# One run of k^T v instead of two, the output weights loaded behind it, and the weight product spread over three q units

## The chip, the cores and the metric

The kernel runs on one core of one Trainium2 chip. The metric is the device time of one execution in microseconds (us), on the slowest core (here the only one). Whole runs of one and the same kernel scatter by about 1 us of 1,624 us.

Some words used throughout: PE is the tensor engine (matmul), PEld its weight loads, DVE the vector engine, ACT the scalar engine, SP the engine that issues all data transfers (DMA) here. PSUM is the memory that matmuls write.

## The reference, cut to what matters

```python
def A(x, wqkv, wo):                      # linear attention, S = 2048, D = 1024, 32 heads of 32
    q, k, v = split(x @ wqkv)
    phi = lambda t: where(t > 0, t + 1, exp(t)) + 1e-6
    kv  = einsum("bhsd,bhse->bhde", phi(k), v)          # one 32 x 32 matrix per head
    den = einsum("bhqd,bhd->bhq", phi(q), phi(k).sum(s)) + 1e-6
    o   = einsum("bhqd,bhde->bhqe", phi(q), kv) / den
    return merge_heads(o) @ wo
def B(x, w_gate, w_up, w_down):          # bilinear block, F = 3584
    return ((x @ w_gate) * (x @ w_up)) @ w_down
# x = x + A(layernorm(x)); x = x + B(layernorm(x)); and both once more (the same weights)
```

## The kernel before: the parts that matter

An attention layer is reordered. v is never computed. Instead G = x^T phi(k) is formed in eight chunks m of 128 rows ("g units", 32 full-size matmuls each), and k^T v is `wv^T G`, done per pair of heads with small matmuls on 64-column tiles of the array ("kv units"). Then M = kv * wo is formed for all heads with 32x32 tiles, in four "quarters" ("weight product"), and the output is q M / den ("out units", 16 full-size matmuls each). A "q unit" is 16 full-size matmuls for one tile of 128 tokens; `div_unit` divides q by den on DVE and turns it with a transposing DMA.

```python
Gs = [GL[:, 2 * D:3 * D], GL[:, 3 * D:4 * D], G3[:], W3[:, 3 * D:4 * D]]
Gs += Gs[0:3] + [pq[7]]                       # eight chunks of G share five places
# ... cut ...
def kv_unit(i):                               # i = 0: chunks 0-3, inside g unit 4; i = 1: chunks 4-7, later
    for m in range(4 * i, 4 * i + 4):
        for c in range(KD):
            for p in (0, 64):
                nc.tensor.matmul(out=acc[0][p:p + 64, c, :], lhsT=wkv[:, m, a:a + 64], rhs=Gs[m][:, a:a + 64], ...)
# ... cut ...  the weight product, in the middle of q units 14 and 15
steps(0, 0, 2);  quarter(0, 0)                # 4 full-size matmuls, then 16 small ones
steps(0, 2, 5);  quarter(0, 1)                # 6, then 16
steps(0, 5, 8);  steps(1, 0, 1);  quarter(1, 0)
phi(q unit 14);  steps(1, 1, 5);  quarter(1, 1)
steps(1, 5, 8);  phi(q unit 15)
# ... cut ...  the order around it (d = division of a tile, g and q = g and q units)
do([g[4]] + d(5, 6) + [q[1], g[5]] + d(7))
load_o(0, 4)                                  # output weights, lower half, 1 MB
load_o(4, 7)                                  # upper half but its last slice
do(d(8) + [q[2], g[6]] + d(9, 10) + [q[3]] + d(11) + [q[4]] + d(12) + [g[7], q[5], kv_unit(1)])
load_o(7, 8)                                  # last slice, 256 KB: its place held chunk 7 of G
last_q_with_m(later)
```

Of the kernel before, what the change touches and what calls it, by code (L numbers as in the profile page):

```python
# [12 lines left out]
F32 = mybir.dt.float32  # L13
# [13 lines left out]
def kernel(  # L27
# [11 lines left out]
    nc = tc.nc  # L39
# [46 lines left out]
    zacc = GL[:, 0:2 * D].bitcast(F32)  # L86
    G3 = const.tile([P, D], BF16, tag="G3", name="G3")

    Gs = [GL[:, 2 * D:3 * D], GL[:, 3 * D:4 * D], G3[:], W3[:, 3 * D:4 * D]]
    Gs += Gs[0:3] + [pq[7]]  # L90
    ring = [rows(R2[:, i * KD * NB:(i + 1) * KD * NB], NB) for i in range(4)]
    ring += [rows(W1[:, i * KD * NB:(i + 1) * KD * NB], NB) for i in range(2)]
    dn = [rows(PQ[0][:], D), rows(PQ[1][:], D), rows(W2[:, 0:4 * D], D), rows(W2[:, 4 * D:8 * D], D),
# [31 lines left out]
    def load_o(a, b):  # L125
        load(rows((W3 if a < 4 else PQ[1])[:], D)[:, a % 4:a % 4 + b - a, :], wo_v[:, a:b, :])
# [30 lines left out]
    def mm_tile():  # L157
        return psum.tile([P, 2, NB], F32, tag="mm", bufs=3, name="ps")
# [15 lines left out]
    def ln_stats(t):  # L174
        st = small.tile([P, 2, 6], F32, tag="st", name="st")
        for c in range(2):
            nc.vector.bn_stats(out=st[:, c, :], in_=X[:, t, c * NB:(c + 1) * NB])  # L177
        mv = small.tile([P, 2], F32, tag="mv", bufs=NT, name="mv")
        nc.vector.bn_aggr(out=mv[:], in_=st[:])  # L179
        ve = small.tile([P, 1], F32, tag="ve", name="ve")  # L180
        nc.gpsimd.tensor_scalar(out=ve[:], in0=mv[:, 1:2], scalar1=1e-5, scalar2=None, op0=ALU.add)  # L181
        rstd = small.tile([P, 1], F32, tag="rstd", bufs=NT, name="rstd")
        nc.gpsimd.tensor_tensor(out=rstd[:], in0=ve[:], in1=mhalf[:], op=ALU.pow)  # L183
        stat[t] = (mv, rstd)
# [11 lines left out]
    def both(ps, lhsT, rhs, start, stop):  # L196
        for n in range(2):
            nc.tensor.matmul(out=ps[:, n, :], lhsT=lhsT, rhs=rhs[:, n * NB:(n + 1) * NB], start=start, stop=stop)  # L198

    def phi(ps, dst, scale, later=None):  # L200
        e = small.tile([P, D], BF16, tag="eb", bufs=3, name="e")
        sc = {} if scale is None else {"scale": scale}
        nc.scalar.activation(out=e[:], in_=flat(ps), func=ACT.Exp, **sc)  # L203
        nc.scalar.activation(out=dst, in_=flat(ps), func=ACT.Relu, **sc)

        def sum_up():
            nc.vector.tensor_scalar(out=e[:], in0=e[:], scalar1=1.0, scalar2=EPS, op0=ALU.min, op1=ALU.add)  # L207
            nc.vector.tensor_tensor(out=dst, in0=dst, in1=e[:], op=ALU.add)

        if later is None:  # L210
            sum_up()
        else:
            later.append(sum_up)

    def layer_A(li):
# [3 lines left out]
        def scale_of(t):  # L219
            return stat[t][1][:] if first and t < TPG else None  # L220
# [14 lines left out]
            return lambda: k_part(t, 0, KD)  # L235

        def q_slot(t):
            return pq[t if t < 8 else t % 4]

        def q_unit(t, later=None):  # L240
            def run():
                ps = mm_tile()
                tl = t % TPG
                for k in range(KD):
                    both(ps, xT[t // TPG][:, k, tl * P:(tl + 1) * P], wq[:, k, :], k == 0, k == KD - 1)
                phi(ps, q_slot(t), scale_of(t), later)
            return run
# [43 lines left out]
        def g_unit(m):  # L291
            def run():
                ps = mm_tile()
                for t in range(NT):
                    both(ps, XN[:, t, m * P:(m + 1) * P], PK[:, t, :], t == 0, t == NT - 1)
                if m == 4:
                    kv_unit(0)()
                nc.scalar.copy(out=Gs[m], in_=flat(ps))
            return run

        acc = []

        def kv_unit(i):

            def run():
                if i == 0:
                    acc[:] = [psum.tile([P, KD, 64], F32, tag="kv0", bufs=1, name="kv")]
                for m in range(4 * i, 4 * i + 4):
                    for c in range(KD):
                        for p in (0, 64):  # L310
                            a = c * P + p
                            nc.tensor.matmul(out=acc[0][p:p + 64, c, :], lhsT=wkv[:, m, a:a + 64],  # L312
                                             rhs=Gs[m][:, a:a + 64], start=(m == 0 and c == 0),
                                             stop=(m == KD - 1), tile_position=(0, p), skip_group_check=True)
                if i == 1:
                    nc.vector.tensor_copy(out=KVb[:], in_=acc[0][:])
            return run

        def last_q_with_m(later):


            qs = [mm_tile(), mm_tile()]
            wide = mm_tile()
            bank = [psum.tile([P, NB], F32, tag=f"kv{i}", bufs=1, name="pm") for i in range(2)]

            def steps(i, a, b):
                t = 14 + i
                tl = t % TPG
                for c in range(a, b):
                    both(qs[i], xT[t // TPG][:, c, tl * P:(tl + 1) * P], wq[:, c, :], c == 0, c == KD - 1)  # L330

            def quarter(h, n, two):
                for i in range(4):
                    for j in range(4):
                        o = bank[j][DH * i:DH * i + DH, :] if j < 2 else two[DH * i:DH * i + DH, j - 2, :]
                        e = DH * (j % 2)
                        nc.tensor.matmul(out=o, lhsT=KVb[DH * j:DH * j + DH, 4 * h + i, e:e + DH],  # L337
                                         rhs=wo[4 * h + i][DH * j:DH * j + DH, n * NB:(n + 1) * NB],
                                         start=True, stop=True, tile_position=(DH * j, DH * i))

                def take(copy, r):
                    cols = slice(n * NB, (n + 1) * NB)
                    if r < 2:
                        copy(out=M[:, 4 * h + r, cols], in_=bank[r][:])
                    else:
                        copy(out=M[:, 4 * h + 2:4 * h + 4, cols], in_=two[:])
                return take

            dve, act = nc.vector.tensor_copy, nc.scalar.copy
            steps(0, 0, 2)  # L350
            take = quarter(0, 0, qs[1])
            take(dve, 0)
            take(dve, 1)
            take(act, 2)
            steps(0, 2, 5)
            take = quarter(0, 1, wide)
            take(dve, 0)
            take(dve, 1)
            take(act, 2)
            steps(0, 5, 8)  # L360
            steps(1, 0, 1)
            take = quarter(1, 0, wide)
            take(act, 0)
            take(act, 1)
            take(dve, 2)
            phi(qs[0], q_slot(14), scale_of(14), later)
            steps(1, 1, 5)
            take = quarter(1, 1, wide)
            take(dve, 0)
            take(dve, 1)  # L370
            take(dve, 2)
            do(later)
            steps(1, 5, 8)
            phi(qs[1], q_slot(15), scale_of(15))

        def out_unit(t):
            def run():
                ps = mm_tile()
                tl = t % TPG
                for c in range(KD):  # L380
                    both(ps, xT[t // TPG][:, c, tl * P:(tl + 1) * P], M[:, c, :], c == 0, c == KD - 1)
                nc.vector.tensor_tensor(out=X[:, t, :], in0=X[:, t, :], in1=flat(ps), op=ALU.add)  # L382
            return run

# [11 lines left out]
        if first:  # L396
# [16 lines left out]
            def take(copy, t, h, a, b):  # L413
                copy(out=xT[0][:, a:b, t * P:(t + 1) * P], in_=pts[t, h][:, a:b, :])  # L414
# [70 lines left out]
        def d(*ts):  # L485
            return [div_unit(t) for t in ts]

        g, q = ([f(i) for i in range(KD)] for f in (g_unit, lambda i: q_unit(8 + i)))
        later = []
        q[5] = q_unit(13, later)  # L490
        do([g[0], g[1]] + d(0) + [g[2]] + d(1, 2) + [g[3]] + d(3) + [q[0]] + d(4))
        do([g[4]] + d(5, 6) + [q[1], g[5]] + d(7))
        load_o(0, 4)
        load_o(4, 7)
        do(d(8) + [q[2], g[6]] + d(9, 10) + [q[3]] + d(11) + [q[4]] + d(12) + [g[7], q[5], kv_unit(1)])
        load_o(7, 8)
        last_q_with_m(later)
        load_gu(0)
        load_gu(1)
        load_gu(2)  # L500
        for j in DN_ORDER[:2]:
            load_dn(j)
        do([out_unit(0)] + d(13) + [out_unit(1), out_unit(2)] + d(14) + [out_unit(3), out_unit(4)] + d(15))
        for j in DN_ORDER[2:6]:
            load_dn(j)
        fill = [lambda t=t: ln_stats(t) for t in range(4)] + [b_norm(t) for t in range(4)]
        do(weave([out_unit(t) for t in range(5, NT)], fill))
        load_dn(DN_ORDER[6])


# [50 lines left out]
    def do(units):  # L561
        for u in units:
            u()
# [80 lines left out]
```

## Time and profile before

| | |
|---|---|
| median of the runs before the prediction | 1623.66 us (1623.50 to 1624.11, 3 runs) |
| span of the profiled run | 1622.4 us |
| PE busy | 99% |
| full-size (128x512) matmuls | 7,424 (28 of them, of the last tile, are cut in two), one start per 0.216 us: an estimated 1,603 us |

From the page of the kernel before: the span, the busy time by engine, and the chain of work that ended last.

```profile
span 1622.4 us, 18054 instructions
PE 1609.2 (99%) x7718; PEld 735.2 (45%) x7869; DVE 615.5 (38%) x941; ACT 283.8 (17%) x383; POOL 54.5 (3%) x135
PE 99%; issue 1%; DMA 0%; DVE 0%; ACT 0%; SPq 0%
```

PE is busy nearly always and the chain never leaves it. What remains to be won is the time in which PE is busy but off its pace of 0.216 us per full-size matmul. The timeline of PE shows it at the first kv unit (columns: start, duration, engine, line, operation, tiles, shapes, count):

```profile
129.14 0.69 PE L312 MATMUL kv<-GL,W 128*64 128x64 bf16 x32
129.67 0.42 PE L312 MATMUL kv<-G,W 128*64 128x64 bf16 x16
129.93 0.42 PE L312 MATMUL kv<-W,W 128*64 128x64 bf16 x16
130.28 3.63 PE L198 MATMUL ps<-W,xT 128*128 128x512 bf16 x15
```

The same kernel's second half of k^T v, from the timeline, starts at 168.37:

```profile
168.37 0.69 PE L312 MATMUL kv<-GL,W 128*64 128x64 bf16 x32
```

Records of the trace carry nanoseconds, and starts are worth more than durations (ends of matmuls are modelled). From them: the last full-size matmul before a kv unit starts 0.309 us ahead of the first small one, 0.093 more than the pace; two small ones take 0.0317 us, the first two 0.053 (0.049 is the step from the second start to the third); from the last small one to the first full-size one it is 0.128 us, and the step after that is 0.226. A half of k^T v (32 pairs) so costs 1.24 us, of which about 0.22 us is for going in and out.

The second quarter of the weight product starts with a wait; the timeline before, PE:

```profile
172.24 0.47 PE L337 MATMUL pm<-W,KVb 32*32 32x512 bf16 x2
172.34 0.39 PE L337 MATMUL ps<-W,KVb 32*32 32x512 bf16 x2
```

The first group lasts 0.47 us instead of 0.39: its second matmul starts 0.097 us after the first instead of 0.003. In the timeline of DVE the copies of the first quarter's two banks run from 170.99 to 172.28 us: the second matmul waits for DVE to empty its bank.

**The measure used from here on.** Whole runs scatter more than the change is worth, so I measure a stretch in each attention layer: from the start of the first matmul of the first g unit to the start of the first matmul of the first out unit. It holds everything that the change reorders ahead of the output stage. In the kernel before, these are the four starts, from the timeline of PE (first layer, then second):

```profile
91.06 1.24 PE L198 MATMUL ps<-R,R 128*128 128x512 bf16 x5
178.40 0.81 PE L198 MATMUL ps<-R,xT 128*128 128x512 bf16 x3
896.70 1.03 PE L198 MATMUL ps<-R,R 128*128 128x512 bf16 x4
984.03 0.81 PE L198 MATMUL ps<-R,xT 128*128 128x512 bf16 x3
```

With the records' nanoseconds both stretches are 87.339 us.

### The profile page before, as it was taken

The numbers are of one execution on the slowest core, as the hardware profiler recorded it, in microseconds if no ns is written. First come the engines' busy times: TensorE is split into PE (matmuls) and PEld (weight loads), VectorE is DVE, ScalarE is ACT, GpSimd is POOL, SyncE is SP. The second block draws the span as 40 slices with busy tenths as digits, with TensorE's granted clock in tenths as the row PEclk, the third lists the DMA queues.
The fourth block names the chain that finished last, engine by engine and source line by source line (L and its number), as shares of the span: only waits on it lengthen the run. The fifth ranks groups of instructions, "written<-read, shape, count | busy, mean of one in ns | idle before, by whom it ended". The sixth has DMA issues, their size and how long they took to land.

```text
span 1622.4 us, 18054 instructions
## 1 busy us (share of the span) xinstructions
PE 1609.2 (99%) x7718; PEld 735.2 (45%) x7869; DVE 615.5 (38%) x941; ACT 283.8 (17%) x383; POOL 54.5 (3%) x135
## 2 busy tenths in 40 slices
PE   9999999999999999999999999999999999999999
PEld 4444444444444444444444444444444444444444
DVE  6799853212311321243245798432123113211111
ACT  5523201101110110011045222011011101101110
POOL 2100000000000000010000000000000000000000
PEclk9999999999999999999999999999999999999999
DMA  7324856511650452142420349555235406511400
GB/s 233 59 72 98 241 162 175 162 53 55 167 168 0 141 160 89 52 155 63 90 56 1 78 98 252 156 163 163 71 101 172 130 20 175 162 65 65 156 0 26
DMA packets 235775, 182.84 MB, mean 113 GB/s; under 512 B 101296, under 2 KB 216496, under 8 KB 235696
## 3 DMA queue, kind: packets, MB, share of 16 engines
q1 hardware_dynamic: 235696, 181.69, 38.9%
q8 instruction: 61, 1.00, 0.3%
q14 instruction: 18, 0.15, 0.0%
HBM read 153.09 MB, written 4.19 MB: 97 GB/s over the span
## 4 chain that ended last, share of the span: by engine, by line
PE 99%; issue 1%; DMA 0%; DVE 0%; ACT 0%; SPq 0%
PE ps L198 50%; PE ps L529 47%; PE ps L556 1%; PE kv L312 0%; DMA X<-in_A_x_dram 0%; PE pm L337 0%; ACT junk L422 0%; PE pt L411 0%; SPq L109 0%; DVE R L398 0%; DVE xT L414 0%; DVE X L537 0%; PE ps L337 0%
## 5 line engine op out<-in xcount | busy, mean ns | idle before, releaser
L529 PE MATMUL ps<-xT,R 128*128 128x512 bf16 x2380 | 525.8, 379 | 2.8
L529 PEld LDWEIGHTS <-R 128*128 128x128 bf16 x2432 | 237.9, 98 | 287.0
L533 DVE TENSOR_TENSOR R<-gs,ps 128x512 bf16<-128x512 f32 x224 | 154.0, 687 | 533.4 <-ACT gs L532 533.4
L198 PEld LDWEIGHTS <-R 128*128 128x128 bf16 x2248 | 220.0, 98 | 265.2
L532 ACT COPY gs<-ps 128x512 f32<-128x512 f32 x224 | 131.3, 586 | 1040.2 <-PE ps L529 1017.2
L529 PE MATMUL ps<-xT,W 128*128 128x512 bf16 x1134 | 250.6, 379 | 0.9
L198 PEld LDWEIGHTS <-xT 128*128 128x128 bf16 x1536 | 149.2, 98 | 180.6 <-issue 2.1
L198 PE MATMUL ps<-W,xT 128*128 128x512 bf16 x996 | 223.1, 379 | 2.3 <-DMA W<-in_A_wqkv_dram 0.4
L529 PEld LDWEIGHTS <-W 128*128 128x128 bf16 x1152 | 112.7, 98 | 135.9
L198 PE MATMUL ps<-W,R 128*128 128x512 bf16 x732 | 170.1, 379 | 0.8
L537 DVE TENSOR_TENSOR X<-X,ps 128x1024 bf16<-128x1024 bf16 (+3 forms) x34 | 39.4, 1159 | 335.7 <-PE ps L198 282.6
L198 PE MATMUL ps<-PQ,R 128*128 128x512 bf16 x486 | 111.6, 379 | 0.6
L198 PE MATMUL ps<-R,R 128*128 128x512 bf16 x506 | 111.8, 379 | 0.4
L198 PE MATMUL ps<-R,xT 128*128 128x512 bf16 x502 | 110.3, 379 | 0.5
L177 DVE BATCH_NORM_STATS2 st<-X 128x6 f32<-128x512 bf16 x128 | 81.9, 682 | 2.1 <-DMA X<-in_A_x_dram 1.9
L203 ACT ACTIVATE e<-ps 128x1024 bf16<-128x1024 f32 x56 | 57.4, 1025 | 140.2 <-PE ps L198 134.7
L181 POOL TENSOR_SCALAR ve<-mv 128x1 f32<-128x1 f32 x64 | 16.8, 262 | 1328.1 <-DVE mv L179 1328.1
L198 PE MATMUL ps<-GL,R 128*128 128x512 bf16 x241 | 57.6, 379 | 0.2
L198 PE MATMUL ps<-xT,R 128*128 128x512 bf16 x240 | 57.5, 379 | 0.2
L382 DVE TENSOR_TENSOR X<-X,ps 128x1024 bf16<-128x1024 bf16 x32 | 38.5, 1212 | 25.5 <-PE ps L198 25.5
L188 DVE TENSOR_SCALAR R<-X,mv,rstd 128x1024 bf16<-128x1024 bf16 x64 | 33.9, 542 | 24.0 <-POOL rstd L183 24.0
L207 DVE TENSOR_SCALAR e<-e 128x1024 bf16<-128x1024 bf16 x64 | 27.0, 422 | 40.0 <-ACT e L203 40.0
(65 smaller groups left out, 446.6 us busy)
## 6 DMA issues: line engine op xcount, KB each, us to landing
R<-in_B_w_gate_dram SPq DMA_DIRECT2D x38, 1024.0 KB, 5.5
R<-in_B_w_up_dram SPq DMA_DIRECT2D x38, 1024.0 KB, 7.4
W<-in_B_w_gate_dram SPq DMA_DIRECT2D x18, 1024.0 KB, 5.4
W<-in_B_w_up_dram SPq DMA_DIRECT2D x18, 1024.0 KB, 7.3
W<-in_A_wqkv_dram SPq DMA_DIRECT2D x10, 1024.0 KB, 6.0
W<-in_B_w_down_dram SPq DMA_DIRECT2D x6, 1024.0 KB, 11.1
PQ<-in_B_w_down_dram SPq DMA_DIRECT2D x4, 1024.0 KB, 7.9
X<-in_A_x_dram SPq DMA_DIRECT2D x15, 256.0 KB, 6.3
```

The costliest lines, as they stand in the source:

```text
L177: nc.vector.bn_stats(out=st[:, c, :], in_=X[:, t, c * NB:(c + 1) * NB])
L181: nc.gpsimd.tensor_scalar(out=ve[:], in0=mv[:, 1:2], scalar1=1e-5, scalar2=None, op0=ALU.add)
L188: nc.vector.tensor_scalar(out=dst, in0=X[:, t, :], scalar1=mv[:, 0:1], scalar2=rstd[:], op0=ALU.subtract, op1=ALU.mult)
L198: nc.tensor.matmul(out=ps[:, n, :], lhsT=lhsT, rhs=rhs[:, n * NB:(n + 1) * NB], start=start, stop=stop)
L203: nc.scalar.activation(out=e[:], in_=flat(ps), func=ACT.Exp, **sc)
L207: nc.vector.tensor_scalar(out=e[:], in0=e[:], scalar1=1.0, scalar2=EPS, op0=ALU.min, op1=ALU.add)
L382: nc.vector.tensor_tensor(out=X[:, t, :], in0=X[:, t, :], in1=flat(ps), op=ALU.add)
L529: nc.tensor.matmul(out=ps[:, n, :], lhsT=w[:, k, j * P:(j + 1) * P], rhs=xT[g % 2][:, k, :], start=(k == 0), stop=(k == KD - 1))
L532: nc.scalar.copy(out=gs[:], in_=ps[:, 0, :])
L533: nc.vector.tensor_tensor(out=hT[:, f, :], in0=gs[:], in1=ps[:, 1, :], op=ALU.mult)
L537: nc.vector.tensor_tensor(out=X[:, t, a:b], in0=X[:, t, a:b], in1=ps, op=ALU.add)
L556: nc.tensor.matmul(out=ps[:, 0, 0:b - a], lhsT=hT[:, f, tl * P:(tl + 1) * P], rhs=wd[f][:, a:b], start=(f == 0), stop=(f == KF - 1))
```

## The change

Its intent: go into and out of the small-tile mode once for k^T v instead of twice, and give the copies out of PSUM more time between quarters. For one run, all eight chunks of G must be kept at once, so four of them go into W3, where the lower half of the output weights was loaded early. That half is now loaded behind k^T v and used last: the quarters run in the order upper half, lower half. The quarters are spread over q units 13, 14 and 15, and the division of tile 12 moves into the output stage.

```diff
-    Gs = [GL[:, 2 * D:3 * D], GL[:, 3 * D:4 * D], G3[:], W3[:, 3 * D:4 * D]]
-    Gs += Gs[0:3] + [pq[7]]
+    Gs = [GL[:, 2 * D:3 * D], GL[:, 3 * D:4 * D], G3[:]] + [W3[:, i * D:(i + 1) * D] for i in (0, 2, 3, 1)] + [pq[7]]
 ... cut: kv_unit(0), kv_unit(1) become kv_run over all eight chunks ...
-            steps(0, 0, 2)          quarter(0, 0)     (copies shared out between DVE and ACT)
-            steps(0, 2, 5)          quarter(0, 1)
-            steps(0, 5, 8); steps(1, 0, 1)   quarter(1, 0)
-            steps(1, 1, 5)          quarter(1, 1)     steps(1, 5, 8)
+            steps(13, 0, 7)         quarter(1, 0)
+            steps(13, 7, 8); steps(14, 0, 4)  quarter(1, 1)
+            steps(14, 4, 8)         quarter(0, 0)
+            steps(15, 0, 6)         quarter(0, 1)     steps(15, 6, 8)
 ... cut: out units start with M's upper half ...
-        load_o(0, 4)
         load_o(4, 7)
-        do(d(8) + [q[2], g[6]] + d(9, 10) + [q[3]] + d(11) + [q[4]] + d(12) + [g[7], q[5], kv_unit(1)])
+        do(d(8) + [q[2], g[6]] + d(9, 10) + [q[3]] + d(11) + [g[7], q[4], kv_run])
         load_o(7, 8)
+        load_o(0, 4)
 ... cut ...
-        do([out_unit(0)] + d(13) + [out_unit(1), out_unit(2)] + d(14) + [out_unit(3), out_unit(4)] + d(15))
+        do([o[0]] + d(12) + o[1:3] + d(13) + o[3:5] + d(14) + o[5:7] + d(15))
 ... cut: down weights 2-5 are issued after the norms of the next layer instead of before them; these norms are
 ... placed anew among the out units; q units 14 and 15 write to the places of G's chunks 0 and 1 ...
```

(The lines of the quarters are condensed; one `steps` of c to d is twice d - c full-size matmuls.)

More of the change, by code (lines that the diff above doesn't have):

```diff
@@ L237, in q_slot @@
         def q_slot(t):
-            return pq[t if t < 8 else t % 4]
+            return Gs[t - 14] if t > 13 else pq[t if t < 8 else t % 4]
         def q_unit(t, later=None):
@@ L295, in run @@
                     both(ps, XN[:, t, m * P:(m + 1) * P], PK[:, t, :], t == 0, t == NT - 1)
-                if m == 4:
-                    kv_unit(0)()
                 nc.scalar.copy(out=Gs[m], in_=flat(ps))
             return run
-        acc = []
-        def kv_unit(i):
-            def run():
-                if i == 0:
-                    acc[:] = [psum.tile([P, KD, 64], F32, tag="kv0", bufs=1, name="kv")]
-                for m in range(4 * i, 4 * i + 4):
-                    for c in range(KD):
-                        for p in (0, 64):
-                            a = c * P + p
-                            nc.tensor.matmul(out=acc[0][p:p + 64, c, :], lhsT=wkv[:, m, a:a + 64],
-                                             rhs=Gs[m][:, a:a + 64], start=(m == 0 and c == 0),
-                                             stop=(m == KD - 1), tile_position=(0, p), skip_group_check=True)
-                if i == 1:
-                    nc.vector.tensor_copy(out=KVb[:], in_=acc[0][:])
-            return run
@@ L319, in last_q_with_m, with kv_run @@
-        def last_q_with_m(later):
-            qs = [mm_tile(), mm_tile()]
+        def kv_run():
+            acc = psum.tile([P, KD, 64], F32, tag="kv0", bufs=1, name="kv")
+            for m in range(KD):
+                for c in range(KD):
+                    for p in (0, 64):
+                        a = c * P + p
+                        nc.tensor.matmul(out=acc[p:p + 64, c, :], lhsT=wkv[:, m, a:a + 64], rhs=Gs[m][:, a:a + 64],
+                                         start=(m == 0 and c == 0), stop=(m == KD - 1), tile_position=(0, p),
+                                         skip_group_check=True)
+            nc.vector.tensor_copy(out=KVb[:], in_=acc[:])
@@ L323, in last_q_with_m, with steps @@
+        def last_q_with_m(later):
+            qs = {}
+            def steps(t, a, b):
+                if a == 0:
+                    qs[t] = mm_tile()
+                tl = t % TPG
+                for c in range(a, b):
+                    both(qs[t], xT[t // TPG][:, c, tl * P:(tl + 1) * P], wq[:, c, :], c == 0, c == KD - 1)
+            steps(13, 0, 7)
             wide = mm_tile()
             bank = [psum.tile([P, NB], F32, tag=f"kv{i}", bufs=1, name="pm") for i in range(2)]
-            def steps(i, a, b):
-                t = 14 + i
-                tl = t % TPG
-                for c in range(a, b):
-                    both(qs[i], xT[t // TPG][:, c, tl * P:(tl + 1) * P], wq[:, c, :], c == 0, c == KD - 1)
@@ L332, in quarter @@
-            def quarter(h, n, two):
+            def quarter(h, n):
+                cols = slice(n * NB, (n + 1) * NB)
                 for i in range(4):
                     for j in range(4):
-                        o = bank[j][DH * i:DH * i + DH, :] if j < 2 else two[DH * i:DH * i + DH, j - 2, :]
+                        o = bank[j][DH * i:DH * i + DH, :] if j < 2 else wide[DH * i:DH * i + DH, j - 2, :]
                         e = DH * (j % 2)
                         nc.tensor.matmul(out=o, lhsT=KVb[DH * j:DH * j + DH, 4 * h + i, e:e + DH],
-                                         rhs=wo[4 * h + i][DH * j:DH * j + DH, n * NB:(n + 1) * NB],
+                                         rhs=wo[4 * h + i][DH * j:DH * j + DH, cols],
@@ L339, in quarter @@
                                          start=True, stop=True, tile_position=(DH * j, DH * i))
-                def take(copy, r):
-                    cols = slice(n * NB, (n + 1) * NB)
-                    if r < 2:
-                        copy(out=M[:, 4 * h + r, cols], in_=bank[r][:])
-                    else:
-                        copy(out=M[:, 4 * h + 2:4 * h + 4, cols], in_=two[:])
-                return take
-            dve, act = nc.vector.tensor_copy, nc.scalar.copy
-            steps(0, 0, 2)
@@ L351, in last_q_with_m @@
-            take = quarter(0, 0, qs[1])
-            take(dve, 0)
-            take(dve, 1)
-            take(act, 2)
-            steps(0, 2, 5)
-            take = quarter(0, 1, wide)
-            take(dve, 0)
-            take(dve, 1)
-            take(act, 2)
-            steps(0, 5, 8)
-            steps(1, 0, 1)
-            take = quarter(1, 0, wide)
-            take(act, 0)
-            take(act, 1)
-            take(dve, 2)
-            phi(qs[0], q_slot(14), scale_of(14), later)
-            steps(1, 1, 5)
@@ L368, in last_q_with_m @@
-            take = quarter(1, 1, wide)
-            take(dve, 0)
-            take(dve, 1)
-            take(dve, 2)
-            do(later)
-            steps(1, 5, 8)
-            phi(qs[1], q_slot(15), scale_of(15))
+                for r in range(2):
+                    nc.vector.tensor_copy(out=M[:, 4 * h + r, cols], in_=bank[r][:])
+                nc.scalar.copy(out=M[:, 4 * h + 2:4 * h + 4, cols], in_=wide[:])
+            quarter(1, 0)
+            steps(13, 7, 8)
+            phi(qs[13], q_slot(13), scale_of(13), later)
@@ L376, in out_unit @@
+            steps(14, 0, 4)
+            quarter(1, 1)
+            do(later)
+            del later[:]
+            steps(14, 4, 8)
+            quarter(0, 0)
+            phi(qs[14], q_slot(14), scale_of(14), later)
+            steps(15, 0, 6)
+            quarter(0, 1)
+            do(later)
+            steps(15, 6, 8)
+            phi(qs[15], q_slot(15), scale_of(15))
         def out_unit(t):
@@ L379, in run @@
                 tl = t % TPG
-                for c in range(KD):
-                    both(ps, xT[t // TPG][:, c, tl * P:(tl + 1) * P], M[:, c, :], c == 0, c == KD - 1)
+                for i in range(KD):
+                    c = (i + 4) % KD
+                    both(ps, xT[t // TPG][:, c, tl * P:(tl + 1) * P], M[:, c, :], i == 0, i == KD - 1)
                 nc.vector.tensor_tensor(out=X[:, t, :], in0=X[:, t, :], in1=flat(ps), op=ALU.add)
@@ L489, in layer_A @@
         later = []
-        q[5] = q_unit(13, later)
+        q[4] = q_unit(12, later)
         do([g[0], g[1]] + d(0) + [g[2]] + d(1, 2) + [g[3]] + d(3) + [q[0]] + d(4))
         do([g[4]] + d(5, 6) + [q[1], g[5]] + d(7))
+        load_o(4, 7)
+        do(d(8) + [q[2], g[6]] + d(9, 10) + [q[3]] + d(11) + [g[7], q[4], kv_run])
+        load_o(7, 8)
         load_o(0, 4)
-        load_o(4, 7)
-        do(d(8) + [q[2], g[6]] + d(9, 10) + [q[3]] + d(11) + [q[4]] + d(12) + [g[7], q[5], kv_unit(1)])
-        load_o(7, 8)
-        last_q_with_m(later)
+        do(later)
+        last_q_with_m([])
         load_gu(0)
@@ L502, in layer_A @@
             load_dn(j)
-        do([out_unit(0)] + d(13) + [out_unit(1), out_unit(2)] + d(14) + [out_unit(3), out_unit(4)] + d(15))
+        o = [out_unit(t) for t in range(NT)]
+        do([o[0]] + d(12) + o[1:3] + d(13) + o[3:5] + d(14) + o[5:7] + d(15))
+        fill = [lambda t=t: ln_stats(t) for t in range(4)] + [b_norm(t) for t in range(4)]
+        do([o[7]] + fill[0:1] + [o[8]] + fill[1:2] + [o[9]] + fill[2:4] + [o[10]] + fill[4:6] + [o[11]] + fill[6:8] + o[12:])
         for j in DN_ORDER[2:6]:
             load_dn(j)
-        fill = [lambda t=t: ln_stats(t) for t in range(4)] + [b_norm(t) for t in range(4)]
-        do(weave([out_unit(t) for t in range(5, NT)], fill))
         load_dn(DN_ORDER[6])
```

## The prediction

> **What bounds the kernel now.** The tensor engine. The page gives PE 99% busy and a chain of work that is 99% PE. In the timeline a 128x512 matmul starts every 0.216 us; the program has 7,424 of them, an estimated 1,603 us of the 1,622.4 us span. The change removes no matrix product (15,740 PE rows in both instruction orders). Only the few us in which PE misses this pace can be won, around k^T v and the weight product, once in each of two attention layers.
>
> **Costs there (timeline, first layer, 128 to 131 and 168 to 177 us).**
> - k^T v runs as two halves of 64 small matmuls. The last full-size matmul starts 0.309 us ahead of the first small one; a pair takes 0.032 us, the first 0.049; coming back takes 0.128 us and one step of 0.226. A half costs 1.24 us. The Trainium skill, "TensorEngine Tiling (Array Packing)", Key Properties, says that changing the tiling mode drains the engine; this trace agrees, about 0.2 us in and out.
> - A quarter of the weight product costs 0.47 us; four before, four after.
> - In the second quarter PE waits 0.09 us for the vector engine to empty a bank of the first (0.097 us between two small matmuls that normally start 0.003 apart), in both layers.
>
> **What the change does to PE.**
> - One k^T v run: 2.25 instead of 2.47 us (estimate: one entry, one exit, 64 pairs). Gain 0.22 us a layer.
> - Eight or more full-size matmuls between quarters instead of six: copies end before the next quarter. Gain 0.09.
> - The first quarter now uses the upper half of the output weights, whose last slice (256 KB) is loaded only after k^T v, with 14 matmuls between. Before, it landed 3.0 and 3.8 us after issue, 0.2 to 0.7 us ahead of use. Now I estimate use 3.3 us after the last small matmul starts and landing at 3.3: a tie. Loss 0 to 0.2, say 0.05.
> - The lower half (1 MB, 5.7 us to landing before) is also loaded behind k^T v, used about 8.1 us later: in time by 1 us or more.
> - The first output unit takes the PSUM buffer of q unit 14, freed an estimated 0.8 us before. No loss.
> - Division of tile 12 moves into the output stage, 4.3 us of DVE work. PE needs 3.45 us per output unit, three PSUM buffers give slack, the transposes are needed over 20 us later. No loss. Gate and up weights start loading about 5 us earlier; they were not late.
>
> **Sum.** 0.22 + 0.09 - 0.05 = 0.26 us a layer, 0.5 us in all, 0.03%: all on the critical path, but the size of the runs' spread. Predicted 1623.1 us, range 1621.9 to 1624.3. Faster by over 2%: 0.005; within 2%: 0.99; slower by over 2%: 0.005.
>
> **What would show it.** Timeline: one run of 128 small k^T v matmuls, about 2.0 us from first to last start, near 164 us, none near 129; no 0.09 us gap inside a quarter. Waits: PE waiting for an output-weight DMA means the tie was lost; DVE adds of the output stage holding PE would show the moved division costs.
>
> **What would make it wrong.** Weight loads landing over 0.5 us late; a PSUM buffer freed later than estimated, stalling the first output unit; a transpose held behind 8 MB of weights.

## The result

| | before | after |
|---|---|---|
| median | 1623.70 us (6 runs) | 1623.60 us (6 runs) |
| range | 1623.10 to 1624.11 | 1623.08 to 1624.32 |
| span of the profiled run | 1622.4 | 1621.9 |

The ratio is 0.9999, 95% interval 0.9987 to 1.0012: the same. (Ratios are the mean time of one kernel's fast runs over that of the other's of the same rounds, so not quite the ratio of the medians.) The whole runs cannot tell +0.5 from -0.5 us, so the trace has to.

From the page of the changed kernel:

```profile
span 1621.9 us, 18193 instructions
PE 1617.3 (100%) x7869; PEld 735.5 (45%) x7869; DVE 613.1 (38%) x941; ACT 284.9 (18%) x383; POOL 54.3 (3%) x135
PE 99%; DMA 0%; DVE 0%; issue 0%; SPq 0%
```

More busy time and more instructions do not mean more work: the trace of the kernel before lacks 151 of its 7,869 matmul records, the new trace lacks none. The first layer's k^T v in the timeline of the changed kernel, PE:

```profile
163.15 0.69 PE L305 MATMUL kv<-GL,W 128*64 128x64 bf16 x32
163.68 0.42 PE L305 MATMUL kv<-G,W 128*64 128x64 bf16 x16
163.93 1.18 PE L305 MATMUL kv<-W,W 128*64 128x64 bf16 x64
164.94 0.42 PE L305 MATMUL kv<-PQ,W 128*64 128x64 bf16 x16
165.30 3.19 PE L197 MATMUL ps<-W,xT 128*128 128x512 bf16 x14
```

One run of 128 small matmuls in 2.02 us between first and last start, as intended. The four ends of the stretch, changed kernel, timeline of PE:

```profile
90.54 1.03 PE L197 MATMUL ps<-R,R 128*128 128x512 bf16 x4
177.55 0.81 PE L197 MATMUL ps<-R,xT 128*128 128x512 bf16 x3
895.84 1.03 PE L197 MATMUL ps<-R,R 128*128 128x512 bf16 x4
983.44 0.81 PE L197 MATMUL ps<-R,xT 128*128 128x512 bf16 x3
```

That is 87.015 us in the first layer (0.324 less) and 87.600 us in the second (0.261 more), together 0.063 us less. From there on nothing else moved: from the first out unit of the first layer to its B layer 55.254 before and 55.253 after; from there to the second stretch 663.039 in both; from the second stretch to the last matmul 635.427 and 635.426. The other 0.5 us between the two spans arose before the first g unit (91.064 against 90.537 us), in code that the change does not touch.

What the second layer lost is in the list of waits of the changed kernel; the kernel before has no such lines (columns: who <- for what: us in all, times, longest):

```profile
PEld L332 <- DMA W<-in_A_wo_dram: 0.8, 1, 0.8
PE pm L332 <- DMA W<-in_A_wo_dram: 0.3, 1, 0.3
```

and in its timeline, at the third quarter of the second layer, the first to use the lower half of the output weights:

```profile
979.14 0.14 PEld L332 LDWEIGHTS <-KVb 32*32 32x32 bf16 x16 [0.81 <-DMA W<-in_A_wo_dram]
979.14 0.39 PE L332 MATMUL pm<-W,KVb 32*32 32x512 bf16 x2 [0.32 <-DMA W<-in_A_wo_dram]
```

By starts, PE lost 0.386 us here (0.695 from the last full-size matmul instead of 0.309). A second loss is not in the list of waits: inside the first quarter of that layer the 13th small matmul, the first to use the last slice of the weights, started 0.198 us after the 12th instead of 0.003. In the timeline of the changed kernel the quarter falls into two parts:

```profile
973.76 0.39 PE L332 MATMUL ps<-PQ,KVb 32*32 32x512 bf16 x2
973.97 0.39 PE L332 MATMUL pm<-PQ,KVb 32*32 32x512 bf16 x2
```

It is missing from the waits because the matmuls before it were, by their modelled ends, still busy. 0.195 + 0.386 = 0.581, and 87.015 + 0.581 = 87.596 of the 87.600 us.

The transfers themselves, view of DMA issues in a window of the second layer and in one of the first (columns: tile <- source, engine, operation, count, KB, us from issue to landing), changed kernel:

```profile
W<-in_A_wo_dram SPq DMA_DIRECT2D x1, 1024.0 KB, 7.9
PQ<-in_A_wo_dram SPq DMA_DIRECT2D x1, 256.0 KB, 3.2
```

and the first layer:

```profile
W<-in_A_wo_dram SPq DMA_DIRECT2D x1, 1024.0 KB, 6.9
PQ<-in_A_wo_dram SPq DMA_DIRECT2D x1, 256.0 KB, 2.8
```

Before the change, the lower half took this long, with about 20 us to spare (same view, kernel before, early in the first layer):

```profile
W<-in_A_wo_dram SPq DMA_DIRECT2D x1, 1024.0 KB, 5.7
```

So the gain came as costed in both layers, and the second layer gave it back by waiting for loads that now stand behind k^T v. Two questions were left: is that the whole reason, and why does the same load take 5.7, 6.9 and 7.9 us?

### The profile page after: what moved, and what is told of

Read it like the earlier page. It is cut to its first block, busy times and chain, and to the rows that moved or that the text cites. A ratio compares the mean times of both kernels' runs of the same rounds, so it can differ in the third digit from the quotient of the medians.

```text
span 1621.9 us, 18193 instructions
## 1 busy us (share of the span) xinstructions
PE 1617.3 (100%) x7869; PEld 735.5 (45%) x7869; DVE 613.1 (38%) x941; ACT 284.9 (18%) x383; POOL 54.3 (3%) x135
## 4 chain that ended last, share of the span: by engine, by line
PE 99%; DMA 0%; DVE 0%; issue 0%; SPq 0%
PE ps L197 50%; PE ps L511 48%; PE ps L538 1%; DMA W<-in_A_wo_dram 0%; PE kv L305 0%; PE ps L167 0%; PE pm L332 0%; PE pt L391 0%; DVE xT L394 0%; SPq L108 0%; DVE X L519 0%; DVE xT L162 0%; PE ps L332 0%
```

## The experiments

All gave correct results. "Stretch" is the measure above, in us.

| trace | first layer | second layer | waits of PE for output weights in it |
|---|---|---|---|
| before | 87.339 | 87.339 | none |
| before_again | 87.338 | 87.336 | none |
| after | 87.015 | 87.600 | second layer: 0.195 slice, 0.386 lower half |
| after_again | 87.015 | 87.273 | second layer: 0.258 slice |
| after_third | 87.644 | 87.084 | first layer: 0.625 lower half; second: 0.069 slice |
| merge_only | 87.114 | 87.114 | none |
| eight_runs (seven, see there) | 88.461 | 88.461 | none |
| strips | 87.014 | 87.017 | none |
| strips_again | 87.015 | 87.016 | none |
| shift_fetch | 87.017 | 87.963 | second layer: 0.942 lower half |
| late_division | 87.016 | 87.017 | none |
| alone | 87.016 | 87.016 | none |
| both_clear | 87.016 | 87.186 | second layer: 0.171 slice |

"Slice" is the wait inside the first quarter for the last 256 KB, "lower half" the wait ahead of the third quarter for the 1 MB.

### after_again, after_third: the changed kernel as it is

> The changed kernel once more, unchanged. The measure, here and in all runs, is the stretch from the first x^T k matmul to the first matmul of the output stage, in each of the two attention layers: 87.339 and 87.339 us in the kernel before, 87.015 and 87.600 in the changed kernel, whose second layer lost 0.195 us inside the first quarter and 0.386 us ahead of the third, waiting for output weights. Theory A (the weights behind k^T v have no slack, and how late they are is chance of the DMA): the first layer within 0.05 us of 87.015 or a little longer, the second different from 87.600 by over 0.1 us. Theory B (something at a fixed place in the program of the second layer delays them): 87.015 and 87.600 again, within 0.05 us. Whole kernel: ratio 1.000, as the start of the kernel alone scatters by 0.5 us.

> The changed kernel a third time, unchanged: 87.015 us in the first layer; in the second between 87.2 and 87.6: the wait inside the first quarter 0.15 to 0.3 us (it came twice), the wait ahead of the third quarter 0 to 0.4 us (it came once).

The first repeat gave 87.015 and 87.273, the second 87.644 and 87.084. Neither theory A nor B was right alone: the slice is late in the second layer in three of three looks (0.195, 0.258, 0.069 us) and never in the first, which points to something at a fixed place; the lower half was late once in the second layer, once in the first and once not at all, which looks like chance. The timeline of after_third shows the wait in the first layer, which the third expectation had excluded:

```profile
174.51 0.39 PE L332 MATMUL pm<-W,KVb 32*32 32x512 bf16 x2 [0.56 <-DMA W<-in_A_wo_dram]
```

Summed over both layers, the changed kernel won 0.063, 0.390 and -0.050 us in the three looks, of the 0.647 it would win without waits. Whole kernel, five rounds: median 1623.19 against 1623.72 of before, ratio 0.9998 (0.9986 to 1.0011), the same.

### merge_only: the merged run alone

The edit, against the kernel before. Chunk m of G is written where nothing is needed any more: g unit m has just read the columns m*128 to m*128+127 of the normalised input for all tokens, and nobody reads them again.

```diff
+        Gs = [XN[:, 8:16, m * P:(m + 1) * P] for m in range(KD)]
-                if m == 4:
-                    kv_unit(0)()
-                nc.scalar.copy(out=Gs[m], in_=flat(ps))
+                nc.scalar.copy(out=Gs[m], in_=flat(ps).rearrange("p (c e) -> p c e", e=P))
...
-        do(d(8) + [q[2], g[6]] + d(9, 10) + [q[3]] + d(11) + [q[4]] + d(12) + [g[7], q[5], kv_unit(1)])
-        load_o(7, 8)
+        do(d(8) + [q[2], g[6]] + d(9, 10))
+        load_o(7, 8)
+        do([q[3]] + d(11) + [q[4]] + d(12) + [g[7], q[5], kv_unit(0), kv_unit(1)])
```

> The kernel before with k^T v in one run and nothing else of the change; x^T k lies in dead strips of the normalised input, so that the output weights need not wait and land early. If one pair of mode switches costs 0.226 us: 87.113 us in both layers (87.339 - 0.226). The 0.09 us wait inside the second quarter stays. If the merge gains nothing by itself: 87.339. If the late weights have nothing to do with the loss of the second layer: the second layer longer than the first.

87.114 in both layers: 0.225 us less than before. One entry and exit is worth 0.225 us, as costed. The wait inside the second quarter is still there (0.098 us between its first two matmuls), and the timeline of merge_only shows the same 0.47 us group as before:

```profile
170.97 0.47 PE L333 MATMUL pm<-W,KVb 32*32 32x512 bf16 x2
```

### eight_runs: more entries and exits

```diff
-                if m == 4:
-                    kv_unit(0)()
+                if m >= 2:
+                    kv_unit(m - 2)()          # one chunk per run
...
-        ... [g[7], q[5], kv_unit(1)])
+        ... [g[7], kv_unit(6), q[5], kv_unit(7)])
```

> The kernel before with k^T v cut into eight runs of 16 small matmuls (x^T k in strips, weights early). If each run costs one entry and one exit, 0.226 us, whatever its length: six more runs, 87.339 + 1.36 = 88.70 us in both layers. If the cost hangs on the number of small matmuls and not on the switches: 87.34.

The kernel was not what I wrote: `kv_unit(6)` follows `kv_unit(5)`, which stands at the end of g unit 7, with nothing between, so the trace shows seven runs, not eight. Against the kernel before, which has two, that is five more, and the stretch grew by 1.122 us: 0.224 us per entry and exit. The cost is one per run, whatever its length (16 to 128 matmuls), and not per small matmul.

### strips: the changed kernel with all output weights early

The same places for G as in merge_only, in the changed kernel; nothing is left that makes the weights wait.

```diff
-    Gs = [GL[:, 2 * D:3 * D], GL[:, 3 * D:4 * D], G3[:]] + [W3[...] for i in (0, 2, 3, 1)] + [pq[7]]
+        Gs = [XN[:, 8:16, m * P:(m + 1) * P] for m in range(KD)]
...
+        load_o(0, 4)
         load_o(4, 7)
-        do(d(8) + [q[2], g[6]] + d(9, 10) + [q[3]] + d(11) + [g[7], q[4], kv_run])
-        load_o(7, 8)
-        load_o(0, 4)
+        do(d(8) + [q[2], g[6]] + d(9, 10))
+        load_o(7, 8)
+        do([q[3]] + d(11) + [g[7], q[4], kv_run])
```

> The changed kernel with x^T k in dead strips of the normalised input, and all output weights loaded before k^T v. If the second layer lost its time to the late output weights: 87.015 us in both layers (87.339 - 0.226 - 0.094 - 0.004), no wait of PE for output weights, 0.6 us less than the changed kernel over the whole kernel, 0.65 us less than before (ratio 0.9996, inside the noise of whole runs). If the second layer is slower for another reason (DMA load, instruction fetch on PE's side): 87.015 and about 87.6.

> The kernel with x^T k in dead strips once more: 87.015 us in both layers within 0.005, as nothing in it waits for a weight load, whatever the instruction packets do.

87.014 and 87.017, then 87.015 and 87.016: every look and both layers within 3 ns. The ends of the stretch in the timeline of strips, second layer:

```profile
895.73 1.03 PE L195 MATMUL ps<-R,R 128*128 128x512 bf16 x4
982.75 0.59 PE L195 MATMUL ps<-R,xT 128*128 128x512 bf16 x2
```

This shows that the late weights were the whole reason for the second layer's loss. It is also the version that beats both: 0.647 us less than before over the two stretches. Five rounds, on one chip with after_again: median 1622.94 against 1623.72 of before and 1623.19 of the changed kernel; ratio to before 0.9995 (0.9981 to 1.0009). By whole runs alone this too is "the same"; the gain is shown by the trace. Against merge_only it gains 0.099 us a layer. The two kernels differ in all the rest of the change, but the gain is the size of one gap that is gone: the first two matmuls of the second quarter are 0.003 us apart again, and not 0.098.

### shift_fetch: moving the instruction packets

The traces list a second kind of transfer beside the kernel's own: packets of the instruction queue, 16 KB each, one per 256 PE instructions. The Trainium skill, "Runtime: NRT & Kernel Launch", Instruction fetch mechanics, says that an engine's instructions are refilled in 16 KiB blocks of 256 through a DMA queue of its own, at a cost "mostly hidden"; the spacing in this trace agrees (61 such packets for about 15,700 PE instructions). No wait of PE for one shows: in every trace of the changed kernel and its variants a stretch is 87.01 to 87.02 us plus the waits for output weights in the table. But k^T v issues 256 PE instructions in 2 us, so one such packet always falls into or just behind it, next to the loads.

```diff
             idle(9)
+            for _ in range(74):
+                nc.tensor.matmul(out=zps[:, 0, 0:32], lhsT=xT[3][:, 0, 0:P], rhs=xT[3][:, 0, 0:32], start=True, stop=True)
```

> The changed kernel with 74 tiny matmuls (148 PE instructions) added at the start, before any data is used. In the traces a 16 KB packet of the instruction queue comes once per 256 PE instructions; in the second layer it fell into the transposes of tile 11 (landed 5.1 to 5.3 us after issue, others 3.04) and the first quarter then waited 0.2 to 0.26 us for the last slice of the output weights, in the first layer it came just after them and nothing waited. Theory B (the fetch delays the transposes and the slice queued behind them): the shift moves it away in the second layer and into the transposes in the first, so the inner wait changes sides: 0 in the second layer, about 0.2 us in the first, whose tile 11 lands over 4 us after issue. Theory A (chance, or the second layer itself): the second layer goes on losing 0.2 us or more inside the first quarter, the first nothing. The start of the kernel gets longer by some us, which the stretch measured leaves out.

Half right. The transposes of tile 11 changed as theory B said: in the first layer they took 4.52 us to land (3.04 before the shift), in the second 3.66 (5.1 to 5.3). In the second layer the wait inside the first quarter was gone. But it did not appear in the first layer (the slice landed 2.82 us after issue), so late transposes do not by themselves make the slice late. And the lower half landed 8.3 us after issue in the second layer and cost PE 0.942 us, which neither theory had said. View of DMA issues, shift_fetch, second layer, then first:

```profile
W<-in_A_wo_dram SPq DMA_DIRECT2D x1, 1024.0 KB, 8.3
PQ<-in_A_wo_dram SPq DMA_DIRECT2D x1, 256.0 KB, 2.9
```

and the first layer:

```profile
W<-in_A_wo_dram SPq DMA_DIRECT2D x1, 1024.0 KB, 5.9
PQ<-in_A_wo_dram SPq DMA_DIRECT2D x1, 256.0 KB, 2.8
```

### late_division: no transposes ahead of the loads

```diff
-        do(... + [q[3]] + d(11) + [g[7], q[4], kv_run])
+        do(... + [q[3], g[7], q[4], kv_run])
...
-        do([o[0]] + d(12) + o[1:3] + d(13) + o[3:5] + d(14) + o[5:7] + d(15))
+        do([o[0]] + d(11) + o[1:2] + d(12) + o[2:4] + d(13) + o[4:6] + d(14) + o[6:7] + d(15))
```

> The changed kernel with the division of tile 11 also moved into the output stage, so that no transposes are under way when the last slice of the output weights is loaded. If transposes stretched by the fetch carry the delay: the slice lands 2.9 us or less after issue in both layers, no wait inside the first quarter. 87.015 in both layers unless the lower half (1 MB) lands over 7.4 us after issue, as it did once. If the fetch delays the slice itself: the wait of 0.2 us in the second layer stays.

The slice landed 2.86 and 2.63 us after issue and nothing waited: 87.016 and 87.017, as the first theory said. Yet the lower half landed 7.2 us after issue in the first layer, again without transposes anywhere near.

### alone: no load behind the output weights

```diff
-        load_gu(0)
-        load_gu(1)
-        load_gu(2)
-        for j in DN_ORDER[:2]:
-            load_dn(j)
         o = [out_unit(t) for t in range(NT)]
-        do([o[0]] + d(12) + o[1:3] + ...
+        do([o[0]] + d(12))
+        load_gu(0)
+        ... the other loads ...
+        do(o[1:3] + ...
```

> The changed kernel with the gate and up weights issued after the first output unit and tile 12, so that no load follows the output weights closely. If the following loads take DMA time from the lower half of the output weights (landed 6.9, 7.0 us after issue in the first layer, 7.9 and 5.8 in the second): it lands within 5.9 us of issue in both layers, over 1.3 us ahead of use. If not: 6.9 us again in the first layer. The wait inside the first quarter of the second layer stays at 0.15 to 0.3 us, as the transposes of tile 11 are as before.

This falsified the theory that the lower half is late because the following loads take DMA time from it: it landed 7.3 us after issue in the first layer and 6.3 in the second. The slice did come a little earlier (2.90 us in the second layer) although the transposes of tile 11 took 5.03 us there, and nothing waited; the expected wait of 0.15 to 0.3 us did not come.

### both_clear: a rule put to the test

By now one rule fitted all 12 loads of the lower half in the six traces of the changed kernel and its variants. To test it on new data, the packet of each layer was placed where it should be over before the load is issued:

```diff
+            for _ in range(74):                       # as in shift_fetch
+                nc.tensor.matmul(...)
...
+        if li == 1:                                   # in the first B layer
+            for _ in range(54):
+                nc.tensor.matmul(out=ps[:, 0, 0:32], lhsT=ident[:], rhs=ident[:, 0:32], start=True, stop=True)
```

> A rule read from the traces so far, in 12 of 12 loads of the lower half of the output weights: if the 16 KB instruction packet of PE is still under way when the load is issued, its issue takes 1.1 to 1.4 us and it lands 6.9 to 8.3 us after issue; if the packet is over, 0.43 us and 5.75 to 6.3 us. Here 148 PE instructions are added at the start and 108 more in the first B layer, so that the packet of the first layer comes where that of the second came in the changed kernel, or a little before, and that of the second stays. Rule: in both layers the packet ends before the load is issued (2.70 us after the first small matmul of k^T v), issue 0.43 us, landing 5.7 to 6.4 us, no wait ahead of the third quarter; 87.015 us in the first layer, 87.015 to 87.3 in the second (wait inside the first quarter 0 to 0.26). If it was chance: landing 6.8 to 8.3 us in the first layer, as in five of six looks.

All 14 loads of the lower half; times in us from the records of the trace:

| trace, layer | PE's 16 KB packet under way | load issued at | issue took | landed after issue |
|---|---|---|---|---|
| after, 1 | 165.35 to 166.59 | 165.85 | 1.11 | 6.86 |
| after, 2 | 970.28 to 971.23 | 971.15 | 1.24 | 7.95 |
| after_again, 1 | 165.48 to 166.72 | 165.98 | 1.11 | 6.99 |
| after_again, 2 | 970.08 to 971.04 | 971.28 | 0.43 | 5.80 |
| after_third, 1 | 166.18 to 167.50 | 166.48 | 1.40 | 7.98 |
| after_third, 2 | 970.95 to 972.20 | 972.41 | 0.43 | 6.12 |
| shift_fetch, 1 | 165.99 to 166.87 | 166.89 | 0.43 | 5.87 |
| shift_fetch, 2 | 971.53 to 973.15 | 972.20 | 1.33 | 8.31 |
| late_division, 1 | 165.50 to 166.62 | 165.91 | 1.09 | 7.22 |
| late_division, 2 | 969.68 to 971.05 | 971.21 | 0.43 | 5.75 |
| alone, 1 | 166.06 to 167.01 | 166.03 | 1.35 | 7.33 |
| alone, 2 | 969.94 to 971.00 | 971.33 | 0.43 | 6.32 |
| both_clear, 1 | 165.64 to 166.52 | 166.85 | 0.43 | 6.86 |
| both_clear, 2 | 972.26 to 973.37 | 973.50 | 0.43 | 6.38 |

The issue time obeys the rule in 14 of 14, two of them foretold: 0.43 us when the packet is over, 1.09 to 1.40 us when it is under way during the issue. The landing obeys it less sharply: 5.75 to 6.86 us in the one case and 6.86 to 8.31 in the other, and the 6.86 of both_clear's first layer missed the foretold 5.7 to 6.4. PE waited for the lower half in three of the seven loads that met a packet and in none of the seven that did not. The stretches came out as the rule said: 87.016, and 87.186 with a wait of 0.171 us for the slice. The issue of the load in the timeline of SP (start, duration), changed kernel, first layer:

```profile
165.85 1.11 SPq L108 DMA_DIRECT2D W<-in_A_wo_dram  x1
```

and shift_fetch, which moved the packets, first layer, then second:

```profile
166.89 0.43 SPq L108 DMA_DIRECT2D W<-in_A_wo_dram  x1
972.20 1.33 SPq L108 DMA_DIRECT2D W<-in_A_wo_dram  x1
```

So that a packet under way holds up the issue of this load is shown for six of the seven, also by moving the packet: in these six the issue ended 0.37 to 0.38 us after the packet did. The seventh, the second layer of after, stays open: there the issue went on for 1.16 us after the packet's end. Nor does it hold for every load: the slice, issued just ahead, took 0.34 to 0.36 us to issue in all 14 cases, 12 of them with PE's packet under way. The longer issue is only a part of the late landing: the seven held loads landed 1.36 us later after issue in the mean (7.52 against 6.16), of which 0.80 us is the issue itself. Why the rest is late, and whether it happens on the one DMA engine that carries the packet, is not shown; the trace does not say which engine moved which packet.

What makes the slice late in the second layer (four looks with a wait, three without, across the changed kernel and its variants) stays open: it was late only where the transposes of tile 11 took over 5 us to land and gate and up loads followed closely, and in the looks without one of the two (two without the late transposes, one without the loads) nothing waited. The traces hold a lead that was not tested: the second layer has an 8 KB packet of another instruction queue near this place, the first has none. In the four looks with a wait, and in alone, it was under way when the slice was issued, overlapped PE's packet and took 1.65 to 1.92 us, where the other packets of its kind within the program took 0.31 to 0.95 us; in shift_fetch and late_division it was over before. Whether it delays the others or is itself delayed is not shown.

### before_again: how repeatable the measure is

> The kernel before once more: 87.339 us in both layers within 0.01, if the stretch is as repeatable as it looks; the first x^T k matmul between 90.0 and 91.6 us, as in the other traces, if the scatter of the whole runs comes from the start.

87.338 and 87.336. The first g unit started at 89.989 us, just under the 90.0 that I had expected, and at 91.064 in the first trace: 1.07 us of scatter before the first g unit, in one and the same kernel, with the same code (whether on the same chip, the record does not say; four traces on one chip whose kernels have this start in common, after_again, merge_only, eight_runs and strips, lie between 90.02 and 90.67). That is more than everything the change could win, and enough to hide it in whole runs.

## Why the prediction was right or wrong, point by point

- **The whole time was right**: 1623.1 us predicted with a range of 1621.9 to 1624.3, 1623.60 measured, the same within 2%. It was close mainly because little was at stake: the forecast gain of 0.5 us did not come (0.063 us in the first trace), and the range would have held no change as well.
- **PE bounds the kernel: right.** From the end of one stretch to the next, and to the last matmul, the time was the same to 1 ns.
- **"Gain 0.22 us a layer" for the single run: right.** merge_only 0.225; seven runs 0.224 per entry and exit.
- **"Gain 0.09" for the spread quarters: right.** strips against merge_only 0.099; the gap of 0.097 us inside the second quarter is gone.
- **"A tie. Loss 0 to 0.2, say 0.05" for the last slice: the mechanism was right, the size too small in the second layer.** Three looks lost 0, 0 and 0 in the first layer and 0.195, 0.258 and 0.069 in the second.
- **"In time by 1 us or more" for the lower half: wrong, and this is the step that failed.** The term that failed is the time to landing: I took the 5.7 us of one load at a quiet time for a load behind k^T v, used 8.1 us after the last small matmul. The twelve loads of the lower half that were issued early (before, before_again, merge_only, eight_runs and both strips) took 5.50 to 6.35 us; behind k^T v and the slice it was 5.75 to 6.86 us where PE's instruction packet was over, and 6.86 to 8.31 us where it was under way. So the place behind the slice is the smaller part (6.16 us in the mean without a packet, 5.85 for the early loads); the prediction knew nothing of the packet. The margin was 0.5 us in the first layer and -0.39 in the second in the first trace; PE waited in two of three looks at the changed kernel, for 0.386 and 0.625 us. Together with the slice this gave back 0.58, 0.26 and 0.69 us of the 0.65 us won.
- **"No loss" from the PSUM buffer of the first out unit, and from the division moved into the output stage: right.** In the first trace, the third quarter's wait apart, PE goes on at its pace, and the output stage takes 55.253 against 55.254 us.
- **What would make it wrong** named "weight loads landing over 0.5 us late"; that is what happened (0.625 us of waiting in after_third).

So the expected gain is real, on the critical path, and was spent on a new wait that the same change created. Take the wait away (strips) and 0.65 us of it stays.

## What to carry to other kernels

Merging two runs of small-tile matmuls saves one fixed entry and exit (here 0.225 us) and no more, so count the runs, not the matmuls. When a reordering frees PE time by letting a load start later, price the load by its worst landing at that place (here 8.31 us), and not by one landing in a quiet stretch (5.7); better, look for a place in memory that is dead already, so that the load need not move. When a change is smaller than the scatter of whole runs, measure a stretch between two fixed instructions of the trace: here it repeats to 3 ns, while the start of the kernel alone scatters by 1 us.

## What the Trainium skill lacked or had wrong

- "TensorEngine Tiling (Array Packing)", Key Properties, says that switching the tiling mode drains the engine but gives no cost. Here one run of small-tile matmuls costs 0.225 us beside its matmuls, for entry and exit together.
- "TensorE: Matmul & The Clock Gate", Back-to-back issue gap, gives about 131 ns per matmul for a stream of weight loads and 128x512 matmuls, and calls about 216 ns the isolated case; other sections of the same page measure 215.7 ns back to back. Here such a stream runs at 216 ns from start to start, in all stages after the first matmuls of the kernel and at a granted clock of 1.0: this agrees with those sections, not with the 131 ns.
- "Runtime: NRT & Kernel Launch", Instruction fetch mechanics, calls the cost of a block boundary mostly hidden. For PE no wait shows here, but the skill gives no figure for what a block does to other transfers: the 1 MB load right behind the slice took 1.09 to 1.40 us to issue instead of 0.43 where a 16 KB packet was under way (7 and 7 of 14 loads) and landed after 6.86 to 8.31 us instead of 5.75 to 6.86, while the slice's own issue was not held up.
- No page says that 256 PE instructions issued as small matmuls last only 2 us, so that such a packet falls into or close behind every long run of them.
